# Attention and SwiGLU block: the first queries and keys loaded through two DMA queues instead of one

## Chip, cores, metric

One core of a Trainium2 chip. The metric is device time in microseconds (us) of one execution. The span of a profile runs from the first to the last instruction and is some 1.8 us shorter than the device time of that execution. In the profile's lines PE stands for TensorE's matmuls, PEld for its weight loads, DVE for VectorE, ACT for ScalarE, POOL for GpSimd and SP for SyncE; a q behind the name marks the engine's sequencer, here the issue of a DMA (a load or store), and L93 is line 93 of the kernel. A load "lands" when its completion is seen.

## The reference

```python
q_s = softmax(q, over head_dim);  k_s = softmax(k, over seq)      # 8 batches x 8 heads x 576 x 64, float32
kv  = einsum('bhsd,bhse->bhde', k_s, v)
x   = einsum('bhsd,bhde->bhse', q_s, kv)  -> (4608, 512)
out = (silu(x @ w_gate) * (x @ w_val)) @ w_out                    # d_ff = 1536
```

## The kernel before

The eight batches are handled in turn: attention gives 576 rows of `x`, and the two FFN matmuls run over rows that are ready. The FFN fills TensorE from about 14 us on, and later batches' attention is woven into it. Only the start matters here. A "tile" of queries or keys is four heads (`G` is 0 or 1), two to a partition half, 576 KB:

```python
def load(what, src, b, G, pieces=((0, T),), after=None):
    t_ = ld.tile([128, 2, T * 64], FP32, tag=what, name=what)
    raw[what, b, G] = t_
    for t0, t1 in pieces:                      # one DMA per piece, all on SyncE's queue
        last = nc.sync.dma_start(out=t_[:, :, 64 * t0:64 * t1], in_=head_ap(src, b, G, t0, t1))
        ...
    return last
# ... (cut)
kd = []
for G in range(NG):                            # order: q, k, q, k
    load("q", q, 0, G)
    kd.append(load("k", k, 0, G))
d = nc.gpsimd.dma_start(out=v16[0], in_=head_ap(v, 0, 0))        # values: GpSimd's queue, cast to bf16
tc.add_manual_dep(d.ins, kd[0].ins.name, SYNC, reason="order of loads")
# ... more values; then on the same queue the weight slices wg, wv, wg, wv, ..., wo (four times)
spin(8)                                        # warm-up matmuls on zeros
spin(6, first)                                 # six more, after the first row sums
# ... transpose of q tile 0, then
spin(6)
kv_first(0)                                    # needs the values
# ... (cut)
after = w_dma[0]                               # batch 1's loads wait for the first slice of wo
```

And of batch 1, later in the program, three operations that come into the story: VectorE's multiplication of the first queries by their inverse row sums, and GpSimd's two casts of values. The second cast has an order on VectorE, the first has none:

```python
norm_mul(1, 0)                                 # VectorE, two inputs in SBUF
# ... (cut)
i = norm_mul(1, 1)
cast_v(1, 0)                                   # GpSimd, reads SBUF
c = cast_v(1, 1)
tc.add_manual_dep(c.ins, i.ins.name, SYNC, reason="order of the vector port")
```

The softmax here doesn't subtract the row's maximum and nothing guards it: scores larger than these inputs give would overflow.

## Time and profile before

| | |
|---|---|
| device time, 3 runs | 311.17, 311.33, 312.36 us |
| span of the profile | 309.5 us |
| TensorE busy | 97% of the span |
| end of the second query load | 8.28 us |
| first FFN matmul | 14.17 us |
| from there to 37 us | TensorE full |

How to read it: after the first FFN matmul TensorE has work all the time, so a gain must come out of the first 14 us. The lines are in the prediction.

### The profile page before, as it was taken

The page shows a single profiled execution, that of the slowest core. Times are in us where ns is not written, and L with a number is a line of the kernel's source. Part 1 is how long each engine was busy: PE and PEld are TensorE (multiplying, and loading weights), DVE is VectorE, ACT ScalarE, POOL GpSimd, SP SyncE. Part 2 cuts the span into 40 slices and gives each one's busy share as a digit, 9 for nine tenths or more (in the row PEclk, how much of TensorE's full clock was granted, in tenths as well). Part 3 has the DMA queues.
Part 4 walks back from the last instruction along what each step waited for, and adds up shares of the span by engine and source line. Part 5 has one row for each costly group of instructions (what it writes and reads, how often), then busy time and mean ns, then how long its engine had stood idle before and what let it go on. Part 6 is the DMA issues. An engine that isn't in the chain of part 4 may idle for free.

```text
span 309.5 us, 5442 instructions
## 1 busy us (share of the span) xinstructions
PE 299.9 (97%) x2157; PEld 149.6 (48%) x2182; DVE 161.6 (52%) x286; ACT 146.4 (47%) x214; POOL 32.6 (11%) x39
## 2 busy tenths in 40 slices
PE   6899999999999999999999999999999999999995
PEld 2577745554444444454444444444444444444443
DVE  3844487945754566365826492639353324433421
ACT  5843578785674375447464737455043113312300
POOL 2960021510200110002000200000000000000000
PEclk9999999999999999999999999999999999999999
DMA  7999999999337815590739362605310302020133
GB/s 261 200 194 206 276 386 389 358 217 391 88 74 214 314 34 111 128 385 17 144 73 354 99 125 61 184 0 107 72 35 0 70 11 56 3 68 8 26 71 103
DMA packets 43018, 45.78 MB, mean 148 GB/s; under 512 B 19568, under 2 KB 28272, under 8 KB 42992
## 3 DMA queue, kind: packets, MB, share of 16 engines
q1 hardware_dynamic: 34096, 39.95, 43.6%
q0 software_dynamic: 8752, 5.31, 12.0%
q8 instruction: 17, 0.28, 0.4%
q10 hardware_dynamic: 144, 0.16, 0.2%
q14 instruction: 9, 0.07, 0.1%
HBM read 37.75 MB, written 9.44 MB: 152 GB/s over the span
## 4 chain that ended last, share of the span: by engine, by line
PE 94%; DMA 2%; DVE 1%; issue 1%; ACT 1%; SPq 0%
PE g_ps L289 30%; PE u_ps L289 30%; PE o_ps L322 29%; DMA q<-in_q_dram 2%; PE kv L194 2%; PE xp L250 1%; PE o_ps L343 1%; DVE qs L149 0%; DVE rs L135 0%; PE tp L169 0%; SPq L77 0%; PE xp L207 0%; ACT eq L121 0%; ACT xt L264 0%; DVE o_sb L347 0%
## 5 line engine op out<-in xcount | busy, mean ns | idle before, releaser
L296 ACT ACTIVATE sg<-g_ps 128x512 bf16<-128x512 f32 (+2 forms) x120 | 64.7, 554 | 133.7 <-PE g_ps L289 120.2
L298 DVE TENSOR_TENSOR hr<-sg,u_ps 128x512 bf16<-128x512 bf16 (+3 forms) x120 | 72.6, 617 | 86.8 <-PE u_ps L289 79.9
L289 PE MATMUL g_ps<-xt,wg 128*128 128x512 bf16 (+2 forms) x473 | 110.9, 358 | 0.5
L289 PE MATMUL u_ps<-xt,wv 128*128 128x512 bf16 (+2 forms) x479 | 111.1, 358 | 0.1
L322 PE MATMUL o_ps<-wo,hr 128*128 128x512 bf16 x403 | 92.5, 379 | 1.0 <-issue 0.2
L289 PEld LDWEIGHTS <-wv 128*128 128x128 bf16 x480 | 46.8, 98 | 46.6 <-DMA wv<-in_moe_w_val_dram 0.2
L289 PEld LDWEIGHTS <-wg 128*128 128x128 bf16 x480 | 46.3, 98 | 45.4 <-issue 0.6
L322 PEld LDWEIGHTS <-hr 128*128 128x128 bf16 x420 | 40.9, 98 | 48.6
L110 DVE COPY o_sb<-o_ps 128x512 f32<-128x512 f32 x33 | 22.4, 680 | 39.0 <-PE o_ps L322 35.4
L124 POOL CAST vb<-v 128x1152 bf16<-128x1152 f32 x14 | 17.7, 1267 | 135.8 <-DMA v<-in_v_dram 132.0
L135 DVE TENSOR_REDUCE rs<-eq 128x18 f32<-128x1152 bf16 (+2 forms) x18 | 21.7, 1214 | 13.0 <-ACT eq L121 13.0
L149 DVE TENSOR_TENSOR qs<-eq,rr 128x1152 bf16<-128x1152 bf16 (+2 forms) x18 | 21.7, 1216 | 0.1
L121 ACT ACTIVATE eq<-q 128x1152 bf16<-128x1152 f32 (+2 forms) x18 | 18.3, 1051 | 4.7 <-DMA q<-in_q_dram 4.6
L121 ACT ACTIVATE ek<-k 128x1152 bf16<-128x1152 f32 (+2 forms) x17 | 17.9, 1101 | 0.6 <-DMA k<-in_k_dram 0.6
L296 ACT ACT_TABLE_LOAD x12 | 15.4, 1283 | 0.2
L121 ACT ACT_TABLE_LOAD x11 | 14.1, 1283 | 0.2
L264 ACT CAST xt<-xp 128x512 bf16<-128x512 f32 x14 | 7.8, 587 | 4.2 <-PE xp L250 4.2
L265 DVE CAST xt<-xp 128x512 bf16<-128x512 f32 x14 | 9.0, 683 | 0.7 <-PE xp L250 0.7
L393 PE MATMUL idle<-zero 128*128 128x512 bf16 x20 | 6.4, 474 | 2.9 <-DVE rs L135 1.7
L194 PEld LDWEIGHTS <-ek 64*64 64x64 bf16 x504 | 6.3, 107 | 1.7 <-ACT ek L121 0.4
L194 PE MATMUL kv<-vb,ek 64*64 64x65 bf16 x504 | 6.7, 194 | 0.0
L250 PE MATMUL xp<-qt,kn 64*64 64x512 bf16 (+1 forms) x112 | 6.7, 292 | 0.0
(44 smaller groups left out, 66.5 us busy)
## 6 DMA issues: line engine op xcount, KB each, us to landing
q<-in_q_dram SPq DMA_DIRECT2D x16, 576.0 KB, 5.5
out_dram<-o_sb SPq DMA_DIRECT2D x70, 128.0 KB, 2.3
k<-in_k_dram SPq DMA_DIRECT2D x12, 576.0 KB, 8.1
v<-in_v_dram SPq DMA_DIRECT2D x12, 576.0 KB, 9.3
wo<-in_moe_w_out_dram POOLq DMA_DIRECT2D x4, 384.0 KB, 15.3
k<-in_k_dram SPq DMA_DIRECT2D x4, 320.0 KB, 8.5
k<-in_k_dram SPq DMA_DIRECT2D x4, 256.0 KB, 8.7
v<-in_v_dram SPq DMA_DIRECT2D x2, 320.0 KB, 7.2
```

Of the source, the lines that this page charges most:

```text
L110: eng.tensor_copy(out=out, in_=in_)
L121: nc.scalar.activation(out=e[:, t0:t1], in_=src[:, t0:t1], func=AF.Exp)
L124: return nc.gpsimd.tensor_copy(out=vbs[G][:, :, :, 0:64], in_=raw["v", b, G].rearrange("p h (t d) -> p t h d", d=64),)
L135: i = nc.vector.reduce_sum(out=rs[:, 2 * t0:2 * t1], in_=eq2[:, 2 * t0:2 * t1, :], axis=mybir.AxisListType.X)
L149: last = eng.tensor_mul(qs[:, t0:t1, :].rearrange("p t (h d) -> p (t h) d", d=64), eq2[:, 2 * t0:2 * t1, :], s["rr"][:, 2 * t0:2 * t1].to_ ...
L194: nc.tensor.matmul(out=kv[g][HALF[h], c:c + 65], lhsT=ek[HALF[g], t, h, :], rhs=vbs[G][HALF[g], t, h, :], start=(t == 0), stop=(t == T - 1),)
L250: nc.tensor.matmul(out=o[h][HALF[g], c:c + 64 * (t1 - t0)], lhsT=kn[HALF[h], g, G, :], rhs=qt[G][HALF[h], t0:t1, 64 * g:64 * g + 64], star ...
L265: nc.vector.tensor_copy(out=xt[:, 2 * G + 1, c0:c0 + 512], in_=main[G][1])
L289: nc.tensor.matmul(out=gu[a][i][:, 0:w_], lhsT=(wg, wv)[a][:, kk, ms], rhs=xt[:, kk, c:c + w_], start=(kk == 0), stop=(kk == KT - 1),)
L296: nc.scalar.activation(out=sg[:, 0:w_], in_=g_ps[:, 0:w_], func=AF.Silu)
L298: nc.vector.tensor_mul(hr[:, m, r:r + w1], sg[:, 0:w1], u_ps[:, 0:w1])
L322: nc.tensor.matmul(out=o_ps, lhsT=hr[:, m, r0:r0 + 128], rhs=wo[:, m, :], start=(m == 0), stop=(m == MT - 1),)
```

## The change

Its intent is to bring the first data in sooner. Each of the four first tiles is split by head: one half through ScalarE's queue, the other through SyncE's. The dependency that releases GpSimd's value loads now names SyncE's half of the first keys. A second part cuts the late batches' loads into two pieces: four more DMAs.

```diff
+    def load_first(what, src, G):
+        t_ = ld.tile([128, 2, T * 64], FP32, tag=what, name=what)
+        raw[what, 0, G] = t_
+        for h, eng in ((1, nc.scalar), (0, nc.sync)):
+            ap = bass.AP(tensor=src.tensor, offset=src[0, 4 * G + 2 * h].offset,
+                         ap=[[T * 64, 128], [1, T * 64]])
+            last = eng.dma_start(out=t_[:, h, :], in_=ap)
+        return last
     def load_kv(b):
-        last = b == B - 1
         for G in range(NG):
-            load("k", k, b, G, BANKS if last or (b == B - 2 and G == 1) else whole)
-            load("v", v, b, G, BANKS if last else whole)
+            parts = b >= B - 2 or (b == B - 3 and G == 1)
+            load("k", k, b, G, BANKS if parts else whole)
+            load("v", v, b, G, BANKS if b >= B - 2 else whole)
 ...
         for G in range(NG):
-            load("q", q, 0, G)
-            kd.append(load("k", k, 0, G))
+            load_first("q", q, G)
+            kd.append(load_first("k", k, G))
```

More of the change, by code (lines that the diff above doesn't have):

```diff
@@ L81, in load @@
         return last
+    def load_first(what, src, G):
+        t_ = ld.tile([128, 2, T * 64], FP32, tag=what, name=what)
+        raw[what, 0, G] = t_
+        for h, eng in ((1, nc.scalar), (0, nc.sync)):
+            ap = bass.AP(
+                tensor=src.tensor,
+                offset=src[0, 4 * G + 2 * h].offset,
+                ap=[[T * 64, 128], [1, T * 64]],
+            )
+            last = eng.dma_start(out=t_[:, h, :], in_=ap)
+        return last
     def load_kv(b):
         whole = ((0, T),)
-        last = b == B - 1
         for G in range(NG):
-            load("k", k, b, G, BANKS if last or (b == B - 2 and G == 1) else whole)
-            load("v", v, b, G, BANKS if last else whole)
+            parts = b >= B - 2 or (b == B - 3 and G == 1)
+            load("k", k, b, G, BANKS if parts else whole)
+            load("v", v, b, G, BANKS if b >= B - 2 else whole)
     def w_slice(dst, src, c0, n):
```

## The prediction

> **What bounds the kernel now.** I read the page's chain of work that ended last first, because it says which engine a microsecond must be taken from.
>
> ```profile
> PE 94%; DMA 2%; DVE 1%; issue 1%; ACT 1%; SPq 0%
> ```
>
> TensorE carries 94% of the span. The change touches no matmul, so only the other 6% can move. Next I cut the span into stages with the table of busy time by stretch (columns: stretch, its length, busy us and instruction count of PE, PEld, DVE, ACT, POOL, then granted clock, DMA share, GB/s).
>
> ```profile
> 0.00:14.24 14.24, 9.90 (x145) 4.97 (x146) 8.64 (x25) 9.07 (x16) 8.46 (x17) 1.00 1.05 235
> 14.24:37.00 22.76, 22.76 (x186) 17.95 (x187) 9.88 (x24) 9.87 (x26) 6.49 (x9) 1.00 1.32 210
> 75.00:295.00 220.00, 218.90 (x1339) 101.11 (x1359) 112.64 (x183) 98.46 (x133) 9.23 (x8) 1.00 0.38 105
> ```
>
> From 14.24 us, where the first FFN matmul stands on the chain, PE is full. Before it PE's 9.90 us are largely warm-up matmuls and short attention work: this is the stage that waits for queries and keys of batch 0. So the change is worth whatever it takes off the 14.24 us. The chain of that stretch, in order of time (start, length, what):
>
> ```profile
> 0.74 0.47 SPq L77
> 1.27 0.45 SPq L77
> 1.76 6.52 DMA q<-in_q_dram
> 8.30 0.74 ACT eq L121
> 9.07 1.43 DVE rs L135 x2
> 10.52 0.27 DVE rr L140
> 10.82 1.44 DVE qs L149 x2
> 12.30 0.40 PE tp L169 x4
> 13.77 0.47 PE xp L207 x8
> ```
>
> The second query load (group 1), issued third, ends at 8.28 us; everything behind it follows with gaps of hundredths. Is that load late because of its issue or its bytes? The same table in slices of one microsecond (last column GB/s):
>
> ```profile
> 0.74:1.74 1.00, 0.52 (x2) 0.25 (x3) 0.60 (x7) 1.00 (x1) 0.49 (x2) 1.00 0.00 0
> 1.74:2.74 1.00, 1.00 (x4) 0.34 (x3) 0.00 (x0) 0.48 (x2) 0.00 (x0) 1.00 0.76 157
> 2.74:3.74 1.00, 1.00 (x3) 0.30 (x2) 0.00 (x0) 0.00 (x0) 0.00 (x0) 1.00 1.03 371
> 3.74:4.74 1.00, 0.96 (x3) 0.15 (x1) 0.00 (x0) 0.00 (x0) 0.00 (x0) 1.00 1.04 408
> ```
>
> For one microsecond after the first issue nothing moves, for the next one 157 GB/s, then about 400, with the DMA engines filled (share 1.03, 1.04). It is the bytes that bind, apart from the ramp. Last, the ScalarE instructions that the new DMA issues will stand before, and the vector engine's wait for the second queries:
>
> ```profile
> 0.73 1.28 ACT L370 ACT_TABLE_LOAD   x1 [0.73 <-PEq L596]
> 2.03 0.20 ACT L370 ACTIVATE warm<-warm 128x1 f32<-128x1 f32 x1
> 4.75 1.25 ACT L121 ACTIVATE eq<-q 128x640 bf16<-128x640 f32 x2 [2.51 <-DMA q<-in_q_dram]
> 8.30 1.25 ACT L121 ACTIVATE eq<-q 128x640 bf16<-128x640 f32 x2 [0.94 <-DMA q<-in_q_dram]
> 9.07 1.41 DVE L135 TENSOR_REDUCE rs<-eq 128x10 f32<-128x640 bf16 x2 [0.38 <-ACT eq L121]
> ```
>
> ScalarE idles 2.51 us before the first exp and 0.94 us before the second; VectorE idles only 0.38 us before the second row sums. That last number caps what an earlier second load alone can give.
>
> **What the Trainium skill says.** "DMA: Bandwidth & Descriptors", section "Issuing engines are not separate DMA queues": DMAs started by different engines run on the same 16 DMA engines and interleave; using several only saves the sequencer's issue time. The trace agrees as far as it can: one queue alone reaches 371 to 408 GB/s with full engines, so there is no unused rate after 2.74 us. The same page, section "Queues, rings and completion order": each DMA engine goes round its rows packet by packet, so the two halves of a tile should progress together rather than one after the other; no run here shows that yet. Third, "TensorE: Matmul & The Clock Gate", section "What's actually happening": an idle window of about 3.4 us brings the slow clock. PE's gap between the two warm-up groups is 1.69 us, the granted clock reads 1.00, and the change can only shorten the gap: no risk there.
>
> **The change part by part.**
>
> 1. Four loads of 576 KB (two heads each) become eight of 288 KB, four on SyncE's queue and four on ScalarE's, in the same order q, k, q, k. Bytes and row length (2304 B per partition) stay. An issue takes SyncE 0.45 to 0.47 us. Issues of smaller key pieces later in the trace take 0.37 to 0.40 us, so issue cost hardly falls with size; I take 0.42. Both first issues start at about 0.74 us, each with half the bytes of the first query tile, so its 16 rings are told of all work at about 1.16 instead of 1.21 us. That is nearly nothing.
>
> 2. The ramp. In 1.74 to 2.74 us some 157 KB moved where 400 would have at the later rate: 243 KB missing, 0.6 us at 400 GB/s. Two sequencers handing out descriptors at once can fill part of that. I take somewhat under half: 0.25 us. The rest looks like latency before the first bytes, which a second queue does not shorten. So the first queries arrive at 4.5 instead of 4.74 us, and the second at about 8.0 instead of 8.28.
>
> 3. Behind it. Second row sums wait for min(arrival gain, 0.38 + shift of VectorE's earlier work). With 0.25 us on both loads, VectorE's first group shifts as well and the cap is 0.63: the whole 0.25 us goes through. The values of batch 0 are loaded by GpSimd after SyncE's half of the first keys (the dependency now names that half alone, no later than before), so they shift along. Their last piece, issued at about 8.05 and landing 4.6 us later (12.7), is used from 12.90 on; with a gain of 0.25 it stays just off the path even if it did not move.
>
> 4. ScalarE. Four issues of about 0.45 us with small gaps, 0.73 to about 2.65, now precede the table load (1.28) and the warm-up exp (0.20), which ends near 4.2 us. The first queries come at 4.5: hidden, by 0.3 us. It was hidden by 2.5 before.
>
> 5. The other lines of the diff. Keys and values of the last batches are cut into two pieces: four more issues on SyncE (one for the third last batch, three for the second last). I compared the compiled orders: TensorE, VectorE and GpSimd keep their orders, ScalarE gains its four issues, SyncE the four pieces. Loads and stores share eight completion semaphores in turn; four plus four more is one whole turn, so the final stores keep the numbers they had, and each transfer still waits for the one eight places back. Four issues of 0.4 us lie on a queue which waits for stores in any case, with loads nearly a chunk ahead of use: 0 us.
>
> Sum: 311.33 - 0.25 to 0.3, taken as 311.0 us.
>
> **The rivals.**
>
> A: no gain. The ramp is pure latency and the two queues share what hands out descriptors; then the two half issues serialise, and the second half of each tile is as late as before. For it: the engines are full and the first microsecond is empty. Result 311.2 to 311.5.
>
> B: a loss. ScalarE's issues take longer than SyncE's (its one store issue at the end takes 0.65 us beside SyncE's 0.62), so four take 2.6 us, the table load ends at 4.65 and the warm-up exp at 4.85, past the first queries. Or one queue runs ahead, starts on keys while the other half of the queries is missing, and the exp waits for the slower half. Against: between its first exps ScalarE has 0.94 us idle to give back. Result up to 0.4 us worse, 311.7.
>
> C: a larger gain. The stretch 4.74 to 6.74 also runs at only 318 and 353 GB/s; if one queue is short of outstanding requests there, two would fill it. At 408 the two microseconds would move 145 KB more, 0.35 us. With the ramp that is 0.6, at the cap of part 3: 310.7. Then the gate is no longer the queries but the values and weights on GpSimd's queue, which issues one weight slice per 0.75 us, and an early weight wait of 0.18 us on PE's weight loads would grow.
>
> **Range and chances.** All these lie within 1 us of each other; 2% is 6.2 us, nearly half of the whole starting stage, and no rival reaches it. What widens the range is the clock on the wall: three runs of the kernel before spread from 311.17 to 312.36. I predict 311.0 us, 8 times in 10 between 310.3 and 312.0, and faster by over 2% with 0.01, within 2% with 0.985, slower with 0.005.
>
> **What would show it.** In the changed profile: first exp at about 4.5 us and second query exp at about 8.0 (steps 1, 2); GB/s in the slice after 1.74 well above 157; table load beginning near 2.6 us and the warm-up exp ending before the first queries land (step 4; otherwise rival B); first FFN matmul on the chain at about 14.0 (step 3), with PE as full after it as before; the last stores with the same waits (step 5). The prediction is wrong if the second queries come no earlier, if the first FFN matmul waits for values or weights instead, or if PE shows new waits after 150 us, where the pieces are.

## The result, and the profile after

| | median | runs |
|---|---|---|
| before, same rounds | 311.25 us | 311.08 to 312.63 (6) |
| changed | 311.44 us | 311.05 to 311.92 (6) |

The ratio is 0.9994, with a 95% interval of 0.9972 to 1.0017. A ratio here is the mean time of one kernel's runs over the mean of the other's in the same rounds; so it can lie below 1 while the medians lie the other way, as here, where before has two runs above 312. The time is the same; it lies in the predicted range, but the gain of 0.25 to 0.3 us cannot be seen.

The changed kernel's page, the chain of work that ended last by engine, then its chain in the first stretch in order of time (start, length, what):

```profile
PE 94%; DMA 3%; ACT 1%; issue 0%; SPq 0%; DVE 0%
```

```profile
1.21 4.63 DMA k<-in_k_dram
6.14 5.56 DMA v<-in_v_dram
11.75 0.48 PE kv L429 x36
...
14.16 0.44 PE xp L220 x8
```

The load that gates is now named as that of the values, released by the first keys, and the first FFN matmul stands at 14.53 us, 0.36 later than before. The slices of a microsecond and the late stage, by the same columns as in the prediction:

```profile
1.74:2.74 1.00, 1.00 (x4) 0.34 (x3) 0.00 (x0) 0.00 (x0) 0.00 (x0) 1.00 0.83 182
2.74:3.74 1.00, 1.00 (x3) 0.30 (x2) 0.00 (x0) 0.96 (x1) 0.00 (x0) 1.00 1.03 376
...
75.00:295.00 220.00, 220.00 (x1360) 101.10 (x1358) 112.51 (x183) 98.48 (x134) 9.21 (x8) 1.00 0.39 104
```

The ramp moved 182 instead of 157 GB/s, and then the rate is as before. In the late stage TensorE is full, as before. ScalarE's part:

```profile
0.74 0.42 ACTq L93 DMA_DIRECT2D q<-in_q_dram  x1
2.77 1.28 ACT L383 ACT_TABLE_LOAD   x1 [2.77 <-issue]
4.58 1.25 ACT L134 ACTIVATE eq<-q 128x640 bf16<-128x640 f32 x2 [0.30 <-DMA q<-in_q_dram]
8.49 1.26 ACT L134 ACTIVATE eq<-q 128x640 bf16<-128x640 f32 x2 [1.21 <-DMA q<-in_q_dram]
```

The four issues are hidden, with 0.30 us to spare before the first queries. Those came 0.17 us sooner than in the first profile of before, the second queries 0.19 us later. One more thing differs, in TensorE's timeline, the second group of warm-up matmuls. Before:

```profile
6.39 1.47 PE L393 MATMUL idle<-zero 128*128 128x512 bf16 x6 [1.69 <-DVE rs L135]
```

After:

```profile
6.22 2.74 PE L406 MATMUL idle<-zero 128*128 128x512 bf16 x6 [1.40 <-DVE rs L148]
```

The same six matmuls take nearly twice as long: they start 0.43 us apart in place of 0.22, which I call the slow and the fast clock. The granted clock reads 1.00 in both profiles, so that column does not show this state.

**Theories.** T1: the bytes set the landing, and a second queue adds next to nothing, so there was never a gain to pass on. T2: there is a gain and it is lost: to the slow clock at the start, or given back later. T3: the late pieces cost something. To weigh tenths of a microsecond one profile of each kernel is not enough, so the first two runs repeat both kernels.

### The profile page after: what moved, and what is told of

Read it like the earlier page. It is cut to its first block, busy times and chain, and to the rows that moved or that the text cites. A ratio compares the mean times of both kernels' runs of the same rounds, so it can differ in the third digit from the quotient of the medians.

```text
span 310.0 us, 5484 instructions
## 1 busy us (share of the span) xinstructions
PE 302.3 (98%) x2182; PEld 150.2 (48%) x2182; DVE 161.4 (52%) x286; ACT 146.3 (47%) x214; POOL 33.7 (11%) x39
## 3 DMA queue, kind: packets, MB, share of 16 engines
q10 hardware_dynamic: 720, 1.34, 1.2%
HBM read 37.75 MB, written 9.44 MB: 152 GB/s over the span
## 4 chain that ended last, share of the span: by engine, by line
PE 94%; DMA 3%; ACT 1%; issue 0%; SPq 0%; DVE 0%
PE g_ps L302 30%; PE u_ps L302 30%; PE o_ps L335 29%; DMA v<-in_v_dram 2%; PE kv L207 2%; DMA k<-in_k_dram 1%; PE xp L263 1%; PE o_ps L356 1%; PE tp L182 0%; ACT xt L277 0%; ACT qt L121 0%; PE kv L429 0%; PE xp L220 0%; ACT xt L121 0%; SPq L93 0%
## 5 line engine op out<-in xcount | busy, mean ns | idle before, releaser
L335 PE MATMUL o_ps<-wo,hr 128*128 128x512 bf16 x420 | 93.9, 379 | 0.0
L137 POOL CAST vb<-v 128x1152 bf16<-128x1152 f32 x14 | 18.8, 1345 | 135.7 <-DMA v<-in_v_dram 103.5
L406 PE MATMUL idle<-zero 128*128 128x512 bf16 x20 | 7.8, 555 | 2.6 <-DVE rs L148 1.4
```

Source lines behind the costliest of these rows:

```text
L137: return nc.gpsimd.tensor_copy(out=vbs[G][:, :, :, 0:64], in_=raw["v", b, G].rearrange("p h (t d) -> p t h d", d=64),)
L335: nc.tensor.matmul(out=o_ps, lhsT=hr[:, m, r0:r0 + 128], rhs=wo[:, m, :], start=(m == 0), stop=(m == MT - 1),)
```

## The experiments

Twelve runs followed, two of them repeats, all with correct results, each timed over five rounds. Since the times spread by 0.5 us and more, the verdicts rest on positions in the traces, collected in one table behind the experiments.

### Before, again

> The kernel before, once more, to learn what repeats. All theories: ratio 1.000 within 0.3%. If the landing times of the first loads are a property of the program, the second query tile lands within 0.1 us of 8.28 us again and the values' first tile within 0.2 us of 11.1 us. If they vary from run to run by several tenths, they don't, and one profile can't tell 0.2 us. Theory of the clock phase: the second group of warm-up matmuls (six of them) takes either 1.5 us (fast) or 2.7 us (slow), by chance; in the first profile of this kernel it was fast.

Median 311.71 us against 311.46 of before in the same rounds, ratio 0.9998 (0.9972 to 1.0023). The landing does not repeat: the second query tile landed at 7.76 us instead of 8.28, the values at 10.59 instead of 11.10. That alone, with no change at all, is twice the gain that I had predicted. And yet the span is 309.5 us again. TensorE's timeline shows why:

```profile
13.65 0.66 PE L289 MATMUL g_ps<-xt,wg 128*128 128x320 bf16 x4
...
15.13 0.65 PE L289 MATMUL u_ps<-xt,wv 128*128 128x320 bf16 x4
16.13 1.15 PE L289 MATMUL g_ps<-xt,wg 128*128 128x320 bf16 x8 [0.35 <-DMA wg<-in_moe_w_gate_dram]
```

The first FFN unit starts 0.52 us sooner than in the first profile, but the next unit waits for its weights until 16.13 us, where it stood in the first profile too (16.14). The weights are a second gate, and they ate the whole of this gift.

### Changed kernel, again

> The changed kernel, once more. Ratio 0.998 to 1.002. First theory (the two queues smear the order): second query tile lands again at 8.4 to 8.5 us, 0.2 later than before, although 100 KB more have moved by 7.74 us, and the values again at 11.6 to 11.8. Rival (chance of the run): landing within 0.1 us of 8.28 or earlier, values near 11.1, and the first FFN matmul at 14.0 to 14.2 us instead of 14.60. Theory of the clock phase: the second warm-up group takes 1.5 or 2.7 us by chance.

Median 311.65 us (before 311.46), ratio 0.9996 (0.9973 to 1.002). The second queries landed at 7.92 us this time, the values at 10.73: the later landing of the first profile did not repeat either, so my theory of a smeared order has no support. The clock was slow again, and here it is on the chain:

```profile
4.81 0.74 ACT eq L134
5.58 0.83 DVE rs L148
6.45 2.74 PE idle L406 x6
...
10.17 1.29 PE idle L406 x6
11.46 0.41 PE kv L429 x36
```

The warm-up matmuls themselves hold TensorE until 11.46 us, past the landing of the values; the first FFN matmul starts at 14.18 us. The first output matmul stands at 37.7 us, as in the kernel before. But between 42 us and the end 0.32 us are lost. VectorE's and GpSimd's timelines of this run around 42 us, with columns start, length, instruction:

```profile
41.72 2.20 DVE L162 TENSOR_TENSOR qs<-eq,rr 128x1152 bf16<-128x1152 bf16 x1
```

```profile
41.57 1.14 POOL L137 CAST vb<-v 128x1152 bf16<-128x1152 f32 x1 [20.28 <-DMA v<-in_v_dram]
```

The same two in the first profile of before:

```profile
41.76 1.36 DVE L149 TENSOR_TENSOR qs<-eq,rr 128x1152 bf16<-128x1152 bf16 x1
```

```profile
42.35 1.78 POOL L124 CAST vb<-v 128x1152 bf16<-128x1152 f32 x1 [20.27 <-DMA v<-in_v_dram]
```

Whichever starts second takes longer. When the values of batch 1 land late, the cast starts second and waits (1.78 instead of 1.14 us), which costs nothing; when they land before 41.7 us, it is VectorE's multiplication that waits. From the end of the cast, 42.71, another 1.36 us would give 44.07; the multiplication ended at 43.92. The Trainium skill has this in "SBUF — State Buffer", section "Who interferes with whom": a VectorE instruction with two SBUF inputs and a GpSimd instruction that reads SBUF exclude each other, and the order of issue decides who blocks. The trace agrees, to the 0.15 us between 44.07 and 43.92.

### The split loads alone

> Only the two-queue loads of batch 0; the keys and values of late batches whole as before. My reading of the pieces: they cost and gain nothing, so the ratio is within 0.1% of the changed kernel's. Rival: the pieces keep the turn of the eight completion semaphores at the end as it was, and without them a store or load waits for another: then this is 0.3 us or more slower than the changed kernel, and the difference shows after 200 us.

```diff
 # the changed kernel, with load_kv as in the kernel before
```

Median 311.75 us (before 311.46), ratio 1.0003 (0.9979 to 1.0028). The profile: slow clock, first FFN matmul at 14.18 us, multiplication 2.00 us with the cast started at 41.38. Between 42 and 306 us 0.27 us are lost, but only 0.12 of them behind the multiplication (by 47.4 us); the other 0.15 are lost in batch 2's small matmuls at 59.3 us (0.96 us in place of 0.81), where the trace shows no wait. And a difference at the very end. The compiled order says which of the eight completion semaphores the last two stores use, ScalarE's and SyncE's:

```
before, changed kernel                  6 and 7
split loads alone, late pieces alone    2 and 3
```

At the end of the program SyncE waits for the semaphores one after the other. In the trace each of these waits takes 0.06 us; where the last store is on number 7, nothing is left to do when it lands, and where it is on 3, four waits are. SyncE's drains (its last instructions) began 2.16 us behind the end of the last copy in the kernel before, and 2.40 us in this one. That answers the rival: the pieces bring the turn of the semaphores back to where it was, which saves 0.24 us.

### The late pieces alone

> Only the pieces of the late loads; first loads on one queue as before. My reading: ratio to before within 0.1% of 1, no new wait after 150 us, first FFN matmul at 14.2 us as before. Rival: the pieces cost, 0.3 us or more slower, with waits in the batches 5 to 7.

```diff
 # the kernel before, with load_kv as in the changed kernel
```

Median 311.97 us (before 311.46), ratio 1.001 (0.9987 to 1.0033), six runs from 311.87 to 312.43. Neither expectation holds as written. Nothing happens in batches 5 to 7: between 42 and 306 us the profile keeps the distance to before within 0.01 us. But the start was 0.33 us later by chance (weights at 16.46 us), and the end 0.39 us longer. Of this 0.24 us are the closing waits again, seen in the waits of SyncE's queue at the end (total, times, longest). Before:

```profile
SPq L607 <- DMA out_dram<-o_sb: 0.9, 2, 0.5
```

The pieces alone:

```profile
SPq L607 <- DMA out_dram<-o_sb: 1.2, 2, 0.6
```

The remaining 0.16 us lie between SyncE's last drain and the end of the program, 1.03 instead of 0.87 us. That stretch has two values in the fourteen profiles, 0.87 to 0.90 and 1.02 to 1.05; the longer one in all six that have the late pieces and no edit of the casts, the shorter in the other eight. Why, no run shows.

### Changed kernel with the first cast ordered

> The changed kernel with one more order: GpSimd's cast of batch 1's first values waits for VectorE's multiplication of batch 1's first queries. Theory of the shared port: in the repeat of the changed kernel and in the split alone, weights and so batch 1's values landed earlier, the cast began at 41.4 to 41.6 us, before the multiplication at 41.7, which then took 2.0 to 2.2 us instead of 1.36, and 0.3 us were lost between 42 and 52 us. Here the multiplication takes 1.36 us always and, counted from the start of the first output matmul (about 37.7), the rest is as short as in the kernel before: the delay added between 42 and 60 us is under 0.1 us. Rival (the 0.3 us come from something else, such as the loads or the clock): the delay of 0.25 to 0.3 us stays though the multiplication takes 1.36. In time: 0 to 0.3 us faster than the changed kernel, 311.2 to 311.6 us.

```diff
-        norm_mul(1, 0)
+        n0 = norm_mul(1, 0)
 ...
-        cast_v(1, 0)
+        c0_ = cast_v(1, 0)
+        tc.add_manual_dep(c0_.ins, n0.ins.name, SYNC, reason="order of the vector port")
```

Median 311.25 us (before 311.57), ratio 0.9988 (0.9973 to 1.0002). The multiplication took 1.36 us, and nothing was lost between 42 and 306 us. But this does not test the theory: the values of batch 1 landed at 42.58 us, after the multiplication had begun at 42.07, so the cast would have come second without the order too.

### Changed kernel with a warm-up without a gap

> The changed kernel with a first group of 12 warm-up matmuls instead of 8, so that the matmul engine is busy without a gap from 1.2 us[...]. Theory of the clock phase: the second group takes 1.5 us instead of 2.7 (or the clock rises in the midst of it), the first tiles are turned before 9 us, and the first FFN matmul moves from 14.2 to 14.6 us to 13.7 to 14.0 unless values or weights hold it. Rival (the queries' landing gates the stage whatever the clock): first FFN matmul at 14.2 to 14.5 as in the three profiles with split loads. Second part of the theory: what is gained at the start is partly given back between 42 and 52 us by the cast at the shared port (multiplication of 2.0 us or more). Time 311.1 to 311.6 us.

```diff
-        spin(8)
+        spin(12)
```

Median 311.40 us (before 311.57), ratio 0.9991 (0.9975 to 1.0008). TensorE's timeline:

```profile
1.22 4.84 PE L406 MATMUL idle<-zero 128*128 128x512 bf16 x12 [1.22 <-DVE sel L385]
6.46 1.47 PE L406 MATMUL idle<-zero 128*128 128x512 bf16 x6 [0.40 <-DVE rs L148]
```

The second group is fast. In the trace the distance between the first group's matmuls falls from 0.43 to 0.22 us at about 5.5 us. The first FFN matmul came at 14.21 us, not at 13.7 to 14.0: now the second queries gated it (exp at 8.34 us). With the clock repaired the bytes were the gate, as the rival said. Nothing was given back after 42 us, since the values landed late enough.

### Both repairs on the changed kernel

> Both repairs on the changed kernel: 12 warm-up matmuls first and the ordered cast. If both theories hold: second group fast, first FFN matmul at 13.7 to 14.0 us, first output matmul at 37.2 to 37.5 instead of 37.7 to 38.1, multiplication 1.36 us, and 0.3 to 0.6 us less than the changed kernel: 310.8 to 311.2 us. If weights are a floor (the second slice of the gate weights at 16.1 us), only 0.0 to 0.2 us.

Median 311.16 us (before 311.57), ratio 0.9992 (0.9972 to 1.0012). First FFN matmul 14.09, first output matmul 37.62 instead of 37.75, multiplication 1.36 us, end at 309.35, the shortest span of all: 0.14 us less than before. That is the size expected if the rest is a floor, not the 0.3 to 0.6 us. It has the lowest median, but its interval does not tell it from before.

### Both repairs on the kernel before

> Control: both repairs on the kernel before, first loads on one queue. If the two queues bring something that the two repairs merely uncover, this is 0.2 to 0.4 us slower than the changed kernel with both repairs. If the queues bring nothing, the two are alike within 0.1 us. Against the kernel before: its clock was fast in all three profiles and the cast did not collide, so nothing is repaired and the profile shows the first output matmul at 37.7 us and the end at 309.5.

Median 311.49 us (before 311.57), ratio 1.0000 (0.9979 to 1.0021). First FFN matmul at 13.75 us, thanks to second queries landed at 7.86, but then a wait for the second slice of the value weights, landed at 17.05; first output matmul at 37.74, end at 309.5. As before: a sooner start is worth nothing with one queue, because the weights come no sooner. Against the changed kernel with both repairs the span is 0.15 us longer and the median 0.33 us higher, with intervals that overlap. That lies between the two forecasts (alike within 0.1, slower by 0.2 to 0.4), so the control leaves open whether the two queues bring that much once both repairs are in.

### Batch 1's loads released sooner, without and with the order

> The kernel before, with the loads of batch 1 released by the last slice of the value weights (landing near 30 us) instead of the first slice of the output weights (31.9). Theory of the shared port: batch 1's first values land before 41.7 us, GpSimd's cast starts before VectorE's multiplication of batch 1's first queries (at 41.7 to 41.8) and this takes 1.8 to 2.5 us instead of 1.36; between 42 and 52 us 0.1 to 0.4 us are lost, although every load is earlier. Rival: earlier loads do no harm, the multiplication takes 1.36 and the time from the first output matmul to the end stays 271.75 us or gets shorter. If the values still land after 41.8 us the run tells nothing. Clock phase, by the way: second warm-up group fast as in the other profiles with unsplit loads, or by chance.

> The same, with the cast of batch 1's first values ordered behind that multiplication. Theory of the shared port: the multiplication takes 1.36 us again, and the loss between 42 and 52 us is gone (under 0.05 us), with the same early landing. Rival (the loss comes from the loads themselves): the loss stays.

```diff
-            w_slice(wv, moe_w_val, c0, n)
+            last_w = w_slice(wv, moe_w_val, c0, n)
 ...
-        after = w_dma[0]
+        after = last_w
```

Medians 311.64 and 312.05 us (before 311.34), ratios 1.0006 (0.9991 to 1.0022) and 1.0015 (0.9999 to 1.0031). Both miss their purpose. The loads were issued 2.4 us sooner, but then shared the engines with the output weights, and the values of batch 1 landed at 42.87 us, later than in the kernel before (42.29). So the cast came second:

```profile
42.93 1.30 POOL L124 CAST vb<-v 128x1152 bf16<-128x1152 f32 x1 [21.47 <-DMA v<-in_v_dram]
```

By what was written ahead, the pair tells nothing of the port. In the second one TensorE waited 0.7 us for the output weights. What the pair does tell: the loads compete for bytes here too, and the clock was slow in both, in kernels without split loads (on chip 13, the runs up to here on chip 9). So the slow clock can come without the change; whether the change makes it likelier is taken up below the table.

### All eight halves on SyncE's queue

> The changed kernel with all eight half loads on SyncE's queue. If bytes bind and not issue, the queries and keys land as with two queues: first exp at 4.6 to 4.9, second queries at 7.8 to 8.5 us. If a second queue does fill the ramp, the rate between 1.74 and 2.74 us is 157 to 205 GB/s as in the kernel before instead of 182 to 226, a difference of a few hundredths of a microsecond in time. Rival (issue binds): eight issues of 0.42 us put the last at 4.0 us and the second queries land 0.3 us or more later, over 8.6. Clock phase: if the slow second warm-up group belongs to ScalarE's queue it is fast here (1.5 us); if to the half loads, slow (2.7).

```diff
-        for h, eng in ((1, nc.scalar), (0, nc.sync)):
+        for h, eng in ((1, nc.sync), (0, nc.sync)):
```

Median 314.49 us (before 311.34), ratio 1.0101 (1.0061 to 1.014): slower by 1.0%, clear of the noise though under 2%, and scattered, 312.59 to 317.06. I had not expected this. The first half of the queries landed at 3.87 us, but the rate sank afterwards (slices as above):

```profile
3.74:4.74 1.00, 1.00 (x3) 0.15 (x1) 0.00 (x0) 0.10 (x1) 0.00 (x0) 1.00 1.28 316
4.74:5.74 1.00, 0.08 (x1) 0.00 (x0) 0.34 (x1) 1.00 (x2) 0.00 (x0) 1.00 0.76 182
```

In the second slice only 182 GB/s moved; the six profiles with whole loads have 318 to 394 there. The first keys were whole at 7.30 instead of 6.17 us, the second queries at 8.75, and GpSimd, released by the keys, came late with the values:

```profile
14.04 0.48 PE L429 MATMUL kv<-v,ek 64*64 64x64 bf16 x36 [3.23 <-DMA v<-in_v_dram]
```

The second queries were later than the 8.6 us of the rival. But plain issue time is not the reason: the issues went out every 0.47 us, which at 288 KB each would feed over 600 GB/s. Why halves on one queue run slower than whole tiles on one, or halves on two, stays open. Clock phase: fast, which by what was written ahead speaks for ScalarE's queue and against the half loads.

### Only the first query tile split

> Only the first query tile split over both queues, the other three tiles whole on SyncE's queue, the late pieces as in the changed kernel. If the ramp theory of my prediction has something in it, the first exp starts at 4.4 to 4.5 us, 0.2 us sooner than before, with the other landings alike. What the ten profiles so far suggest: no gain, 4.6 to 4.8 us, as the data of that tile are bound by the rate up to about 4 us. Clock phase: one more sample with one issue on ScalarE's queue.

```diff
 # the changed kernel, with load_first for q of G = 0 only, load for the other three
```

Median 311.75 us (before 311.34), ratio 1.0012 (0.9993 to 1.0031). First exp at 4.74 us, as in the kernel before: no gain. The clock was slow, and TensorE waited again for the last piece of the values, landed at 13.85 us, so the first FFN matmul came at 14.99. Then the cast and the multiplication met again:

```profile
42.54 2.23 DVE L162 TENSOR_TENSOR qs<-eq,rr 128x1152 bf16<-128x1152 bf16 x1
```

The cast had started at 42.43. Another 0.36 us were lost.

### The table

All positions in us, from the traces. "Warm-up": length of the second group. "q1": start of the exp of the second queries. "v": landing of the first values. "wv": landing of the second slice of the value weights. "FFN": first FFN matmul. "mult": start and length of the multiplication of batch 1. "last copy": its start against that of the first profile of before.

| kernel | warm-up | q1 | v | wv | FFN | mult | last copy | span |
|---|---|---|---|---|---|---|---|---|
| before | 1.47 | 8.30 | 11.10 | 17.11 | 14.17 | 41.76, 1.36 | 0 | 309.5 |
| before, again | 1.47 | 7.78 | 10.59 | 16.37 | 13.65 | 41.72, 1.36 | -0.04 | 309.5 |
| late pieces alone | 1.47 | 8.28 | 11.03 | 16.70 | 14.15 | 42.09, 1.36 | +0.33 | 310.2 |
| before, both repairs | 1.47 | 7.88 | 10.67 | 17.05 | 13.75 | 41.77, 1.36 | 0 | 309.5 |
| before, batch 1 sooner | 2.74 | 7.73 | 11.49 | 15.99 | 14.32 | 41.87, 1.36 | +0.23 | 309.7 |
| same, cast ordered | 2.74 | 7.96 | 10.72 | 17.45 | 14.29 | 42.10, 1.36 | +1.25 | 310.8 |
| changed | 2.74 | 8.49 | 11.71 | 16.14 | 14.53 | 42.08, 1.36 | +0.33 | 310.0 |
| changed, again | 2.74 | 8.00 | 10.73 | 15.82 | 14.18 | 41.72, 2.20 | +0.28 | 309.9 |
| split loads alone | 2.74 | 8.32 | 10.29 | 15.28 | 14.18 | 41.73, 2.00 | +0.24 | 310.0 |
| changed, cast ordered | 2.74 | 8.23 | 10.77 | 16.01 | 14.53 | 42.07, 1.36 | +0.31 | 309.8 |
| changed, long warm-up | 1.47 | 8.34 | 10.89 | 15.56 | 14.21 | 41.76, 1.36 | 0 | 309.7 |
| changed, both repairs | 1.47 | 8.22 | 10.87 | 16.32 | 14.09 | 41.64, 1.36 | -0.12 | 309.4 |
| halves on one queue | 1.47 | 8.83 | 13.99 | 18.40 | 17.50 | 45.62, 1.36 | +3.87 | 313.5 |
| first queries split | 2.74 | 7.95 | 10.70 | 16.95 | 14.99 | 42.54, 2.23 | +1.14 | 311.0 |

Five readings of it.

**The landing.** Leaving out the last two rows, six profiles have the loads whole and six have them split. The first exp starts at 4.70 us in the mean with whole loads and at 4.73 with split ones; the second queries' exp at 7.99 and 8.27, with a spread of 0.6 us in the first group and 0.5 in the second. The rate in the slice from 1.74 to 2.74 us is 177 and 200 GB/s in the mean. There is no sooner landing; if anything the second queries come later, by 0.28 us in the mean, with spreads that overlap.

**The chain behind it.** In the six profiles with a fast clock and four tiles alike, the first FFN matmul stands 5.87 us behind the second queries' exp, to 0.01 us, whether split or not. With a slow clock it stands as late as that or later, at 14.18 to 14.53 us, whole or split.

**The clock.** With the old warm-up all five profiles with issues on ScalarE's queue have the slow second group, and two of the six without. So the slow clock does not need those issues; that they make it likelier is suggested by this count of eleven and not shown.

**What the change does move.** GpSimd's value loads, released by half a tile of keys, are issued at 6.22 us in the mean instead of 6.45, and the weights behind them land sooner: the second slice of the value weights at 15.86 instead of 16.78 us, the first slice of the output weights, which releases batch 1's loads, at 31.22 instead of 31.74. The issue alone accounts for 0.23 us of this; the rest is not explained.

**The meeting at 42 us.** In the three profiles in which the cast of batch 1 starts less than 0.4 us ahead of the multiplication, this takes 2.00 to 2.23 us. In the other eleven it takes 1.36. All three are of kernels with split loads, in two of which the sooner weights brought the values of batch 1 to 41.4 and 41.6 us. In the third they came at 42.4, by lateness of the rest. What reaches TensorE is the time added to the multiplication less some 0.51 us that TensorE can spare: 0.64, 0.84 and 0.87 us added cost 0.12, 0.32 and 0.36 us between 42 and 52 us.

The same two kinds of instruction meet in later batches too. Of the 196 multiplications of this size in the fourteen profiles, 15 begin while a cast is under way; where more than 0.15 us of the cast is left, each is longer by that remainder less some 0.15 us, up to 2.35 us. The other 181 take 1.34 to 1.36 us. The 15 include kernels with whole loads (1.69 us at 81.01 us in the repeat of before), so the meeting as such does not need the change.

## Why the prediction was right or wrong

The time was right: 311.44 us, inside the range. That says little for the mechanism, since the range of 310.3 to 312.0 us holds the gain, no gain and the loss alike. The forecast of a small gain was not borne out; what came is my rival A, no gain, by a different mechanism than I gave it. Two of my own signs of being wrong came true in the first profile: the second queries came no earlier, and the chain to the first FFN matmul ran over the values. Of the theories, T1 is what the landings show; the losses of T2 are real, but there was no gain to lose; T3 shows in either part alone and in 0.16 us at the close.

- **What bounds the kernel**: right. In all fourteen profiles the distance to the first profile of before is the same at the last copy as at 71 us, within 0.02 us. Only the first 71 us and the closing differ.
- **Step 1, the issues**: right. They took 0.41 to 0.46 us where I took 0.42, apart from the last at 0.54 and 0.59. My reading behind it was wrong: the key issues of 0.37 to 0.40 us were of whole tiles, and the smaller key pieces of the late batches took 0.42 to 0.50.
- **Step 2, the ramp**: this is the step that failed. I gave the second queue 0.25 us, somewhat under half of the missing 243 KB. The runs show 23 KB more, 0.06 us at 400 GB/s, and nothing of it in the first exp (4.70 and 4.73 us). The line that I had shown held the warning: in that slice the DMA engines were already busy for 0.76 of the time at 157 GB/s, so most of the missing rate was not idle engines. The split raised this share only from 0.73 to 0.86 in the mean. The two halves of a tile did progress together: those of the first queries landed 0.18 us apart in the four profiles that show both, against 0.68 us with all on one queue. The skill sentence that I had quoted, that several issuing engines save only issue time, was the better guide; I overruled it with the word "ramp".
- **Step 3, the chain behind**: half right. With a fast clock the first FFN matmul does follow the second queries by a constant 5.87 us. But a gain there is not passed on whole, since it meets two further gates: the weights, which turned 0.52 us at the first FFN matmul into 0.04 in the repeat of before, and the clock. My rival C had named the weights.
- **"No risk there"**, of TensorE's clock: wrong. Seven of the eleven profiles with the old warm-up have a slow second group, four a fast one. I read the granted clock of 1.00 as proof; it does not show this state. The page that I cited also says that the window of measurement runs freely and that the transition varies from run to run; I had left that sentence unused.
- **Step 4, ScalarE**: right. The table load began at 2.77 us instead of 0.73, the warm-up exp ended at 4.27, 0.30 us ahead of the first queries; rival B did not happen.
- **Step 5, the pieces**: right for the two parts together, and the trace now says what the turn is worth, 0.24 us of closing waits; either part alone loses them. A further 0.16 us at the close goes with the pieces, unexplained.
- **Not foreseen**: that sooner loads can cost. In three profiles with split loads 0.12, 0.32 and 0.36 us went to the cast that took the port first. Shown is the pattern, three of three against none of eleven in batch 1 and the same in later batches, and the arithmetic of the blocking. That the added order cures it is not shown: in none of the runs with the order would the cast have come first.

Still open are the rate of the halves on one queue, the 0.16 us at the close, the cause of the slow clock, and what sets the landing of the second queries anywhere between 7.7 and 8.5 us.

## What to carry to other kernels

Where one queue already fills the DMA engines, as with the whole tiles here, a second one brings no data sooner; look at the rate and at the engines' busy share before looking at queues. When several gates stand within half a microsecond of each other, here queries, values, weights and the warm-up of the clock, moving one was worth nothing by itself, and a load that comes sooner may let another engine take a shared port first: consider ordering such pairs explicitly, a cure that these runs did not put to the test. And repeat the profile of the unchanged kernel before explaining tenths: its landing times moved by 0.5 us on their own.

## What the Trainium skill lacked or had wrong

- "DMA: Bandwidth & Descriptors", section "Issuing engines are not separate DMA queues", says that issuing from several engines saves only sequencer time. Whole tiles on one queue against halves on two bear it out (first exp 4.70 and 4.73 us). For halves on one queue it was not all: with the same eight loads of 288 KB there the rate fell to 182 GB/s between 4.74 and 5.74 us in the one profile, and the kernel took 1.0% longer than before; on two queues it did not (364 to 410 GB/s in that slice, six profiles). The cause is open.
- "TensorE: Matmul & The Clock Gate", section "What's actually happening", gives about 3.4 us of sustained activity as what raises the clock, in a window that runs freely. With that window these runs agree: a first group of eight matmuls, 1.2 to 4.8 us, was not enough in seven of eleven profiles; with twelve the clock rose between 5.5 and 6.4 us in three of three. What it lacks is a word on the profile's granted clock, which read 1.00 in either state here.
- "SBUF — State Buffer", section "Who interferes with whom", is right about the port; a number would help: a multiplication of 128x1152 elements took up to 2.35 us instead of 1.36 when the cast came first, a cast up to 2.36 instead of 1.14 when it came second.
- No page that I read has the closing waits: SyncE takes 0.06 us for each completion semaphore, in turn, so the number that the last store falls on is worth up to 0.24 us in these runs.
